# A column of ones in the rows of x and a new order of the instructions, in an induced attention followed by a rational MLP

## The chip, the cores and the metric

The kernel runs on one core of a Trainium2 chip. The core has five engines with an instruction queue each: TensorE (PE in the rows; its weight loads are PEld), VectorE (DVE), ScalarE (ACT), GpSimd (POOL) and SyncE (SP), which here issues the DMAs. The metric is the device time of one execution in microseconds.

## The reference

Four batches of N = 12,480 tokens with C = 128 channels pass two attentions over m = 32 inducing points and then an MLP with 2,048 hidden units and a rational activation:

```
mab(q, kv): s = (q @ kv.T) / sqrt(C);  a = exp(s - max(s));  a /= a.sum(-1) + 1e-9;  return a @ kv
h   = mab(inducing, x)          # 32 rows for each batch
y   = mab(x, h)                 # 12,480 rows for each batch
z   = y @ w_in                  # 128 -> 2048
g   = (a0 + a1 z + a2 z^2 + a3 z^3) / (1 + |b0| |z| + |b1| z^2 + 1e-6)
out = g @ w_out                 # 2048 -> 128
```

The change is in the first line's first use: the sum over all tokens of exp(s), by which the weighted sum of x is divided.

## The kernel before

The MLP is cut into 832 **units**: 4 batches x 26 blocks of 480 tokens x 8 pieces of 256 hidden units. A unit passes these steps:

- `first` (PE): two matmuls `h<-at,st` into one of three PSUM banks;
- the absolute value: on ACT (`rooms<-h,all`, half of the units), or for the other half, called masked, on DVE (`rooms<-h`, int32), rarely on ACT;
- for a masked unit a constant is added, either on POOL (`l<-rooms,all`, called *pre*) or by two more matmuls on PE (`h<-at,bump`, called *shift*);
- `D` (DVE): a product (`l<-h,all,l` after a pre, `l<-rooms,all,h` otherwise), after which the bank is free;
- a logarithm on ACT (`rooms<-rooms,all`): tile forms of 1,920, 3,840, 5,760 or 7,680 elements, for 1, 2, 3 or 4 pairs of units at once;
- a sigmoid on ACT: into SBUF for one unit or a pair (`rooms<-rooms` of 960 or 1,920), or into a PSUM bank (`i<-rooms`);
- the last product: on DVE (`l<-l,all,i`, when the sigmoid is in PSUM), or an add and a product on POOL;
- `second` (PE): two float32 matmuls `po<-l,w_out`, four records in the trace.

Logarithm and sigmoid have different tables on ACT, so ACT works in **rounds**: load, logarithms of some pairs, load, their sigmoids. `SIZES` says how many pairs each round has.

The attention of batch b + 1 (`induce`, `score`, `weigh`) and of the coming blocks (`tokens`) run beside the units of batch b. `score` of a **group** of four blocks gives the exponentials `e` (`e<-pc,nm` on ACT) and their transposition `eT`. `weigh` then loads the rows of x (`x_rows`, four DMAs `x<-x_t` of 256 KB into the tag `xr`) and on PE adds up, for each of 32 inducing points, exp(s) times x: 16 matmuls `ph<-x,eT` (32 records in the trace), and after them four matmuls `ph<-unit,eT` of one column (8 records), whose moving operand is a column of ones and which give the sums of exp(s) in column C of `ph`. DVE then adds `ph` to `acc`. There are 7 groups for a batch (the last of two blocks).

For batch 0 this runs before the units, in the **opening** (`boot`): there the rows come in nine wide DMAs (`rooms<-x_t`, up to 768 KB), the sums of exp(s) come from `accum_out` of the ACT instruction that makes `e`, and DVE adds them to `acc` in an instruction of their own.

The order of all instructions is fixed when the program is built. `Flow` simulates the engines with the costs of the table `COST` and picks, for each engine, the ready step with the lowest due time, which is its ready time plus a number of `RANK` or `GEN`. Those numbers change along the way: `SETS` has rows of 36 numbers, `PLAN` says which row holds in which of 52 stretches of 16 units. A job like `weigh` tells the planner what its step on an engine takes, by a yield:

```
        yield "bank", 0
        yield "pe", 0.25 * nb
        ph = self.misc(f"ph{b}_{g}")
```

Every engine runs its instructions strictly in this order. Calls of the engines go through a helper, so nearly all rows carry its line, L166; the tiles' names tell them apart.

Of the kernel before, what the change touches and what calls it, by code (L numbers as in the profile page):

```python
# [9 lines left out]
F32 = mybir.dt.float32  # L10
# [3 lines left out]
AF = mybir.ActivationFunctionType  # L14
ALU = mybir.AluOpType
PSUM = bass.MemoryType.PSUM

P = 128
TP = 120
M = 32  # L20
C = 128
HB = 4
BT = HB * TP
# [165 lines left out]
class Flow:  # L189
# [63 lines left out]
    )  # L253
    PLAN = (0, 1, 2, 3, 4, 5, 6, 7, 8, 9, 10, 11, 12, 13, 14, 15, 16, 17, 18, 19, 20, 21, 22, 23, 24, 25, 26, 27, 28, 29, 30, 31, 32, 33, 34, 35, 36, 37, 38, 39, 40, 41, 42, 43, 44, 45, 46, 47, 48, 48, 48, 48,)
    SIZES = (1, 2, 3, 4, 5, 6, 6, 6, 6, 6, 6, 6, 6, 6, 6, 6, 6, 6, 6, 6, 6, 6, 6, 6, 6, 6, 6, 6, 6, 6, 6, 6, 6, 6, 6, 6, 6, 6, 6, 6, 6, 6, 6, 6, 6, 6, 6, 6, 6, 6, 6, 6, 6, 6, 6, 6, 6, 6, 6, 6, 6, 6, 6, 6, 6, 6, 6, 6, 6, 6, 5, 3, 3)
    SWIFT = 8
    TAIL = 0.25
    MERGE = 4
# [1098 lines left out]
```

## Time and profile before

| | |
|---|---|
| time, median of 3 runs | 2217.89 us (2216.58 to 2219.45) |
| the profiled execution: time, span | 2218.13 us, 2216.2 us |
| granted TensorE clock, mean over the span | 0.988 |
| busy share PE, DVE, ACT, POOL | 96%, 92%, 95%, 86% |
| chain that ended last, by engine | PE 49%, DVE 18%, ACT 16%, POOL 9% |

Busy is the time in which an instruction of the engine was under way, as a share of the span. Matmuls are pipelined, so a busy PE may still take more work. An engine's idle time matters only where a later instruction of the chain waits for it.

### The profile page before, as it was taken

The numbers are of one execution on the slowest core, as the hardware profiler recorded it, in microseconds if no ns is written. First come the engines' busy times: TensorE is split into PE (matmuls) and PEld (weight loads), VectorE is DVE, ScalarE is ACT, GpSimd is POOL, SyncE is SP. The second block draws the span as 40 slices with busy tenths as digits, with TensorE's granted clock in tenths as the row PEclk, the third lists the DMA queues.
The fourth block names the chain that finished last, engine by engine and source line by source line (L and its number), as shares of the span: only waits on it lengthen the run. The fifth ranks groups of instructions, "written<-read, shape, count | busy, mean of one in ns | idle before, by whom it ended". The sixth has DMA issues, their size and how long they took to land.

```text
span 2216.2 us, 23881 instructions
## 1 busy us (share of the span) xinstructions
PE 2127.4 (96%) x7722; PEld 1160.0 (52%) x7722; DVE 2044.3 (92%) x2244; ACT 2112.0 (95%) x1640; POOL 1910.9 (86%) x1270
## 2 busy tenths in 40 slices
PE   6889999999999999999999999999999999999998
PEld 3545555555554555555555555555555555555554
DVE  8898999999999989999999999999999999999987
ACT  2799999999999999999999999999999999999997
POOL 0389897899999989997999999998878999999884
PEclk7899999999999999999999999999999999999999
DMA  8121122211111222222112111222110111011000
GB/s 333 51 91 58 60 82 64 65 44 45 45 36 45 75 62 82 64 80 67 45 36 63 46 58 62 73 88 73 56 61 20 45 45 45 27 38 35 27 27 20
DMA packets 76933, 135.13 MB, mean 61 GB/s; under 512 B 13312, under 2 KB 63616, under 8 KB 76800
## 3 DMA queue, kind: packets, MB, share of 16 engines
q1 hardware_dynamic: 76800, 133.52, 19.1%
q8 instruction: 64, 1.05, 0.2%
q14 instruction: 69, 0.57, 0.1%
HBM read 82.59 MB, written 25.56 MB: 49 GB/s over the span
## 4 chain that ended last, share of the span: by engine, by line
PE 49%; DVE 18%; ACT 16%; POOL 9%; issue 6%; DMA 2%; SPq 0%; DVEq 0%; ACTq 0%; POOLq 0%
PE po L166 32%; PE h L166 12%; ACT rooms L166 11%; DVE l L166 11%; POOL l L166 9%; DVE rooms L166 3%; ACT i L166 2%; PE ph L166 2%; ACT L166 2%; DMA rooms<-x_t 1%; PE pc L166 1%; DVE oT L166 1%; PE pd L166 1%; SPq L166 0%; PE pt L166 0%
## 5 line engine op out<-in xcount | busy, mean ns | idle before, releaser
L166 PE MATMUL po<-l,w_out 128*128 128x480 f32 x3328 | 1461.9, 570 | 11.6 <-DVE oT L166 8.1
L166 POOL TENSOR_TENSOR l<-l,rooms 128x960 f32<-128x960 f32 x506 | 1137.5, 2248 | 53.8 <-ACT rooms L166 16.9
L166 PEld LDWEIGHTS po<-l,w_out 128*128 128x128 f32 x3328 | 618.0, 190 | 518.9 <-issue 441.7
L166 DVE SCALAR_TENSOR_TENSOR l<-rooms,all,h 128x960 f32<-128x960 f32 x657 | 780.7, 1205 | 51.7 <-ACT rooms L166 34.1
L166 ACT ACTIVATE rooms<-rooms,all 128x1920 f32<-128x1920 f32 (+3 forms) x278 | 742.0, 2689 | 3.0 <-DVE l L166 2.5
L166 PE MATMUL h<-at,st 128*128 128x480 f32 x1664 | 629.0, 475 | 41.0 <-DVE l L166 37.5
L166 POOL TENSOR_SCALAR l<-l,all 128x960 f32<-128x960 f32 x506 | 543.7, 1075 | 1.7
L166 DVE TENSOR_SCALAR rooms<-h 128x960 int32<-128x960 int32 x413 | 473.2, 1150 | 37.6 <-PE h L166 36.3
L166 ACT ACTIVATE rooms<-rooms 128x1920 f32<-128x1920 f32 (+1 forms) x335 | 461.7, 1402 | 0.2
L166 PEld LDWEIGHTS h<-at,st 128*128 128x128 f32 x1664 | 294.7, 190 | 319.2 <-issue 163.0
L166 ACT ACTIVATE rooms<-h,all 128x960 f32<-128x960 f32 x416 | 433.6, 1052 | 21.6 <-PE h L166 19.8
L166 DVE SCALAR_TENSOR_TENSOR l<-l,all,i 128x960 f32<-128x960 f32 x326 | 385.8, 1206 | 20.5 <-ACT i L166 19.2
L166 ACT ACTIVATE i<-rooms 128x960 f32<-128x960 f32 x326 | 309.0, 964 | 12.7 <-DVE l L166 11.9
L166 POOL TENSOR_SCALAR l<-rooms,all 128x960 f32<-128x960 f32 x175 | 187.5, 1072 | 131.2 <-DVE rooms L166 112.1
L166 DVE SCALAR_TENSOR_TENSOR l<-h,all,l 128x960 f32<-128x960 f32 x175 | 210.6, 1206 | 6.7 <-POOL l L166 5.3
L166 ACT ACT_TABLE_LOAD x146 | 187.3, 1283 | 3.3 <-PEq L1350 0.7
L166 PE MATMUL h<-at,bump 128*128 128x480 f32 x482 | 179.2, 455 | 5.1 <-DVE rooms L166 5.0
L166 PEld LDWEIGHTS h<-at,bump 128*128 128x128 f32 x482 | 86.8, 190 | 78.3 <-DVE rooms L166 41.4
L166 DVE COPY oT<-po 128x480 f32<-128x480 f32 x104 | 67.6, 650 | 20.8 <-PE po L166 20.5
L166 PE MATMUL po<-at,st 128*128 128x480 f32 x104 | 78.5, 755 | 0.0
L166 POOL TENSOR_TENSOR bump<-level,bump 64x128 fp32r<-64x128 f32 x1 | 0.5, 452 | 53.3 <-DVE sum L166 53.3
L166 ACT ACTIVATE e<-pc,nm 128x480 f32<-128x480 f32 (+1 forms) x28 | 18.4, 658 | 24.4 <-DVE nm L166 21.2
(121 smaller groups left out, 763.2 us busy)
## 6 DMA issues: line engine op xcount, KB each, us to landing
xT<-x_c SPq DMA_DIRECT2D x182, 240.0 KB, 3.4
out<-oT SPq DMA_DIRECT2D x104, 240.0 KB, 2.2
at<-hl SPq DMA_DIRECT2D x412, 60.0 KB, 2.0
x<-x_t SPq DMA_DIRECT2D x78, 256.0 KB, 3.4
rooms<-x_t SPq DMA_DIRECT2D x8, 768.0 KB, 13.3
rooms<-x_c SPq DMA_DIRECT2D x5, 960.0 KB, 13.7
raw<-w_in SPq DMA_DIRECT2D x4, 480.0 KB, 8.6
raw<-w_out SPq DMA_DIRECT2D x5, 384.0 KB, 12.5
```

Of the source, the lines that this page charges most:

```text
L166: ins = call(*args, **kw)
```

## The change

The rows of x in DRAM (`x_t`) get a 129th element that is 1, so that a row of four tokens in a partition has 2,064 bytes in place of 2,048. The matmuls `ph<-x,eT` have 129 columns and so also give the sums of exp(s); the matmuls with `unit` and the tile `unit` go, and in the opening `accum_out` and DVE's own instructions for the sums go too. The planner is told another cost for the step. `SETS` and `PLAN` are replaced: 52 rows, one for each stretch, in place of 49; the last rounds of `SIZES` become 6, 2, 4, 3, 2 pairs in place of 6, 5, 3, 3. With that the order of all engines after the opening is another one.

```
     SETS = (
-        (93.1, 124, -262.9, 107.9, -98, -199.3, -83.4, 13.3, 36.9, 113.2, -213.9, 106.7, 409, 149.2, 15.7, 4.9, 67.1, 34.1, -13.5, -190.6, -1.2, 162.6, 30.3, -281.3, 0.07, 0.14, 0.03, 0.09, -1.22, -1.54, 193.8, 106.1, 40, 64.3, 281.9, 30),
+        (93.1, 124, -262.9, 107.9, -135.2, -199.3, -83.4, 13.3, 36.9, 113.2, -213.9, 106.7, 409, 149.2, 15.7, 4.9, 67.1, 34.1, -13.5, -190.6, -1.2, 162.6, 30.3, -281.3, 0.07, 0.14, 0.03, 0.09, -1.22, -1.54, 193.8, 106.1, 45.7, 64.3, 281.9, 30),
...
-        self.unit = cp.tile([P, 1], F32, name="unit")
-        nc.vector.memset(self.unit, 1.0)
...
-            t = self.ap.tile([P, HB, C], F32, tag="xr", name=f"x{b}_{n}", bufs=4)
+            t = self.ap.tile([P, HB, C + 1], F32, tag="xr", name=f"x{b}_{n}", bufs=4)
...
-            nc.scalar.activation(e[rows], pc[rows, 0:BT], AF.Exp, bias=nm[rows], scale=scale, accum_out=sums[rows])
...
+        nc.scalar.activation(e[rows], pc[rows, 0:BT], AF.Exp, bias=nm[rows], scale=scale)
...
-        yield "pe", 0.25 * nb
+        yield "pe", 0.03 + 0.27 * nb
...
-                nc.tensor.matmul(ph[M * j:M * j + M, 0:C], eT[:, c, M * j:M * j + M], xs[j][:, c, :], start=(c == 0), stop=(c == HB - 1))
...
-                V.scalar_tensor_tensor(out=acc[rows, C:], in0=acc[rows, C:], scalar=state[g][rows], in1=sums[rows], op0=ALU.mult, op1=ALU.add)
-            return
-        for c in range(HB):
-            nc.tensor.matmul(ph[rows, C:C + 1], eT[:, c, rows], self.unit[0:TP], start=(c == 0), stop=(c == HB - 1))
-        yield "unring", 0
+                nc.tensor.matmul(ph[M * j:M * j + M, 0:C + 1], eT[:, c, M * j:M * j + M], xs[j][:, c, :], start=(c == 0), stop=(c == HB - 1))
+        if not self.boot:
+            yield "unring", 0
```

In the order of TensorE, the end of the first group's sum of batch 1 (`ph_0`), and the units of block 2 behind it. Before:

```order
L166 MATMUL ph_0_1093<-x_2_1028,eT_0_1018 32x128
L166 MATMUL ph_0_1093<-x_3_1030,eT_0_1018 32x128
L166 MATMUL ph_0_1093<-unit,eT_0_1018 128x1 x4
L166 MATMUL h_2_4_1116<-at_1_1_874,st_645 128x480 x2
L166 MATMUL h_2_5_1121<-at_1_1_874,st_645 128x480 x2
L166 MATMUL po_1_2_1085<-l_1_3_972,w_out 128x480 x2
L166 MATMUL h_2_4_1116<-at_1_1_874,bump 128x480 x2
```

The same place now:

```order
L166 MATMUL ph_0_1077<-x_2_1012,eT_0_1002 32x129
L166 MATMUL ph_0_1077<-x_3_1014,eT_0_1002 32x129
L166 MATMUL h_2_4_1096<-at_1_1_858,st_629 128x480 x2
L166 MATMUL h_2_5_1102<-at_1_1_858,st_629 128x480 x2
L166 MATMUL po_1_2_1069<-l_1_3_956,w_out 128x480 x2
L166 MATMUL h_2_6_1110<-at_1_1_858,st_629 128x480 x2
L166 MATMUL h_2_4_1096<-at_1_1_858,bump 128x480 x2
```

The four matmuls with `unit` are gone, and the shift of unit 2_4 has moved behind the first matmuls of unit 2_6.

In the order of ScalarE, the end of the program: the last two rounds of batch 3's last blocks (`i` is a sigmoid into PSUM). Before:

```order
L166 ACTIVATE i_24_7_14285<-rooms 128x2x480
L166 ACTIVATE i_25_0_14290<-rooms 128x2x480
L166 ACTIVATE i_25_1_14293<-rooms 128x2x480
L166 ACT_TABLE_LOAD
L166 ACTIVATE rooms<-rooms,all 128x5760
L166 ACT_TABLE_LOAD
L166 ACTIVATE i_25_2_14315<-rooms 128x2x480
L166 ACTIVATE i_25_3_14317<-rooms 128x2x480
L166 ACTIVATE i_25_4_14322<-rooms 128x2x480
L166 ACTIVATE i_25_5_14327<-rooms 128x2x480
L166 ACTIVATE i_25_6_14330<-rooms 128x2x480
L166 ACTIVATE i_25_7_14335<-rooms 128x2x480
```

The same place now:

```order
L166 ACTIVATE i_24_7_14195<-rooms 128x2x480
L166 ACTIVATE i_25_0_14198<-rooms 128x2x480
L166 ACTIVATE i_25_1_14203<-rooms 128x2x480
L166 ACTIVATE i_25_2_14206<-rooms 128x2x480
L166 ACTIVATE i_25_3_14212<-rooms 128x2x480
L166 ACT_TABLE_LOAD
L166 ACTIVATE rooms<-rooms,all 128x3840
L166 ACT_TABLE_LOAD
L166 ACTIVATE i_25_4_14229<-rooms 128x2x480
L166 ACTIVATE i_25_5_14233<-rooms 128x2x480
L166 ACTIVATE i_25_6_14236<-rooms 128x2x480
L166 ACTIVATE i_25_7_14241<-rooms 128x2x480
```

The last round has two pairs of units in place of three: the sigmoids of units 25_2 and 25_3 stand a round earlier.

Over the whole program, as the order lists them, these counts change beside those of the sum itself: the logarithms of 1, 2, 3 and 4 pairs from 187, 56, 23 and 12 to 173, 58, 25 and 13; table loads from 146 to 148; sigmoids into SBUF of one unit and of a pair from 164 and 171 to 159 and 175, into PSUM from 326 to 323; matmuls of the shift from 482 to 512; POOL's *pre* from 175 to 160; the absolute value of masked units on ACT from 3 to 1; of ACT's copies out of PSUM (`eT`, `a`, `hl`, `gs`) three, three and two fewer and four more, DVE taking or giving them.

## Rows read from the trace of the kernel before

**Rows 1.** The page: busy time by engine, and one group of weight loads.

```profile
PE 2127.4 (96%) x7722; PEld 1160.0 (52%) x7722; DVE 2044.3 (92%) x2244; ACT 2112.0 (95%) x1640; POOL 1910.9 (86%) x1270
...
L166 PEld LDWEIGHTS po<-l,w_out 128*128 128x128 f32 x3328 | 618.0, 190 | 518.9 <-issue 441.7
```

**Rows 2.** Busy time by stretch; columns PE, PEld, DVE, ACT, POOL, clock, DMA.

```profile
105.00:2204.00 2099.00, 2041.96 (x7204) 1111.34 (x7203) 1955.72 (x1982) 2064.94 (x1572) 1891.06 (x1248) 1.00 0.18 54
```

**Rows 3.** The timeline of PE from 121.5 us: start, length, work.

```profile
122.11 1.08 PE L166 MATMUL ph<-x,eT 120*32 120x128 f32 x32
...
123.12 1.05 PE L166 MATMUL ph<-unit,eT 120*128 120x1 f32 x8
...
124.04 1.12 PE L166 MATMUL h<-at,st 128*128 128x480 f32 x4
```

**Rows 4.** Groups by form on PE: count, busy, mean ns, idle before.

```profile
L166 PE MATMUL ph<-unit,eT 120*64 120x1 f32 x24 | 1.9, 200 | 0.0
...
L166 PE MATMUL h<-at,bump 128*128 128x480 f32 x482 | 179.2, 455 | 5.1 <-DVE rooms L166 5.0
```

**Rows 5.** Groups by form on ACT.

```profile
L166 ACT ACTIVATE rooms<-rooms,all 128x1920 f32<-128x1920 f32 x187 | 350.0, 1894 | 2.8 <-DVE l L166 2.5
...
L166 ACT ACTIVATE i<-rooms 128x960 f32<-128x960 f32 x326 | 309.0, 964 | 12.7 <-DVE l L166 11.9
...
L166 ACT ACTIVATE rooms<-rooms 128x1920 f32<-128x1920 f32 x171 | 304.3, 1795 | 0.2
...
L166 ACT ACTIVATE rooms<-rooms,all 128x3840 f32<-128x3840 f32 x56 | 195.8, 3496 | 0.1
...
L166 ACT ACT_TABLE_LOAD x146 | 187.3, 1283 | 3.3 <-PEq L1350 0.7
...
L166 ACT ACTIVATE rooms<-rooms 128x960 f32<-128x960 f32 x164 | 162.7, 992 | 0.0
...
L166 ACT ACTIVATE rooms<-rooms,all 128x5760 f32<-128x5760 f32 x23 | 117.3, 5099 | 0.1
...
L166 ACT ACTIVATE rooms<-rooms,all 128x7680 f32<-128x7680 f32 x12 | 80.4, 6702 | 0.0
...
L166 ACT ACTIVATE eT<-pt 120x512 f32<-120x512 f32 x10 | 5.9, 592 | 9.4 <-PE pt L166 9.4
```

**Rows 6.** The chain of waits at the end: start, length, work.

```profile
2198.59 0.98 ACT i L166
...
2199.60 1.22 DVE l L166
...
2200.86 10.16 PE po L166 x25
```

**Rows 7.** The timeline of ACT at the end.

```profile
2198.59 5.48 ACT L166 ACTIVATE i<-rooms 128x960 f32<-128x960 f32 x6
```

**Rows 8.** Busy time in the 6 us after each of the 21 groups.

```profile
sum 126.00, PE 124.05 PEld 79.13 DVE 106.22 ACT 119.03 POOL 112.42; mean PE 5.91 PEld 3.77 DVE 5.06 ACT 5.67 POOL 5.35
```

**Rows 9.** Waits of DVE from 105 us: total, times, longest.

```profile
DVE acc L166 <- PE ph L166: 6.9, 9, 1.1
...
DVE l L166 <- PE h L166: 10.4, 19, 2.4
```

**Rows 10.** Groups by form on POOL.

```profile
L166 POOL TENSOR_SCALAR l<-rooms,all 128x960 f32<-128x960 f32 x175 | 187.5, 1072 | 131.2 <-DVE rooms L166 112.1 <-PE h L166 7.2 <-PE po L166 5.2
```

**Rows 11.** Tile x, its transfers.

```profile
DMA to landing us min/median/max: 2.6/3.4/5.0
```

**Rows 12.** The timeline of SP before one group's sum.

```profile
979.13 1.89 SPq L166 DMA_DIRECT2D x<-x_t  x4
```

**Rows 13.** The timeline of PE at that group's sum.

```profile
986.19 1.08 PE L166 MATMUL ph<-x,eT 120*32 120x128 f32 x32
```

**Rows 14.** The chain of waits in the opening.

```profile
10.91 14.03 DMA rooms<-x_t
...
25.02 13.67 DMA rooms<-x_t
```

More of the change, by code (lines that the diff above doesn't have):

```diff
@@ L203 @@
     SETS = (
[49 rows of a table removed]
-    )
-    PLAN = (0, 1, 2, 3, 4, 5, 6, 7, 8, 9, 10, 11, 12, 13, 14, 15, 16, 17, 18, 19, 20, 21, 22, 23, 24, 25, 26, 27, 28, 29, 30, 31, 32, 33, 34, 35, 36, 37, 38, 39, 40, 41, 42, 43, 44, 45, 46, 47, 48, 48, 48, 48,)
-    SIZES = (1, 2, 3, 4, 5, 6, 6, 6, 6, 6, 6, 6, 6, 6, 6, 6, 6, 6, 6, 6, 6, 6, 6, 6, 6, 6, 6, 6, 6, 6, 6, 6, 6, 6, 6, 6, 6, 6, 6, 6, 6, 6, 6, 6, 6, 6, 6, 6, 6, 6, 6, 6, 6, 6, 6, 6, 6, 6, 6, 6, 6, 6, 6, 6, 6, 6, 6, 6, 6, 6, 5, 3, 3)
[52 rows of a table added]
+    )
+    PLAN = (0, 1, 2, 3, 4, 5, 6, 7, 8, 9, 10, 11, 12, 13, 14, 15, 16, 17, 18, 19, 20, 21, 22, 23, 24, 25, 26, 27, 28, 29, 30, 31, 32, 33, 34, 35, 36, 37, 38, 39, 40, 41, 42, 43, 44, 45, 46, 47, 48, 49, 50, 51,)
+    SIZES = (1, 2, 3, 4, 5, 6, 6, 6, 6, 6, 6, 6, 6, 6, 6, 6, 6, 6, 6, 6, 6, 6, 6, 6, 6, 6, 6, 6, 6, 6, 6, 6, 6, 6, 6, 6, 6, 6, 6, 6, 6, 6, 6, 6, 6, 6, 6, 6, 6, 6, 6, 6, 6, 6, 6, 6, 6, 6, 6, 6, 6, 6, 6, 6, 6, 6, 6, 6, 6, 6, 2, 4, 3, 2)
     SWIFT = 8
@@ L695, in x_rows @@
         if self.boot:
-            t = self.mp.tile([P, HB, C], F32, tag=self.place("l"), name=f"x{b}_{n}", bufs=1)
+            t = self.mp.tile([P, HB, C + 1], F32, tag=self.place("l"), name=f"x{b}_{n}", bufs=1)
         else:
-            t = self.ap.tile([P, HB, C], F32, tag="xr", name=f"x{b}_{n}", bufs=4)
+            t = self.ap.tile([P, HB, C + 1], F32, tag="xr", name=f"x{b}_{n}", bufs=4)
         self.nc.sync.dma_start(out=t, in_=self.x_t[b, :, HB * n:HB * n + HB, :])
@@ L702, in x_columns @@
     def x_columns(self, b, n):
-        t = self.ap.tile([C, HB * C], F32, tag="xr", name=f"xT{b}_{n}", bufs=4)[:, 0:BT]
+        t = self.ap.tile([C, HB * (C + 1)], F32, tag="xr", name=f"xT{b}_{n}", bufs=4)[:, 0:BT]
         self.nc.sync.dma_start(out=t, in_=self.x_c[b, :, BT * n:BT * n + BT])
@@ L722, in wide_rows @@
         n, m = 3 * k, min(3, self.NB - 3 * k)
-        t = self.room().rearrange("p a b n -> p (a b n)")[:, 0:m * HB * C].rearrange("p (m h c) -> p m h c", h=HB, c=C)
+        t = self.room().rearrange("p a b n -> p (a b n)")[:, 0:m * HB * (C + 1)].rearrange("p (m h c) -> p m h c", h=HB, c=C + 1)
         self.nc.sync.dma_start(out=t.rearrange("p m h c -> p (m h) c"), in_=self.x_t[b, :, HB * n:HB * (n + m), :])
@@ L755, in score @@
         e = ap.tile([P, BT], F32, tag="e", name=f"e{b}_{g}")
-        if self.boot:
-            state["sum", g] = sums = ap.tile([P, 1], F32, tag="sums", name=f"sums{b}_{g}", bufs=3)
-            nc.scalar.activation(e[rows], pc[rows, 0:BT], AF.Exp, bias=nm[rows], scale=scale, accum_out=sums[rows])
-        else:
-            nc.scalar.activation(e[rows], pc[rows, 0:BT], AF.Exp, bias=nm[rows], scale=scale)
+        nc.scalar.activation(e[rows], pc[rows, 0:BT], AF.Exp, bias=nm[rows], scale=scale)
         yield "free", 0
@@ L784, in weigh @@
             for j in range(nb):
-                nc.tensor.matmul(ph[M * j:M * j + M, 0:C], eT[:, c, M * j:M * j + M], xs[j][:, c, :], start=(c == 0), stop=(c == HB - 1))
-        if self.boot:
-            V, sums = nc.vector, state["sum", g]
-            if g == 0:
-                V.tensor_copy(out=acc[:, 0:C], in_=ph[:, 0:C])
-                V.tensor_copy(out=acc[:, C:], in_=sums)
-            else:
-                V.scalar_tensor_tensor(out=acc[rows, 0:C], in0=acc[rows, 0:C], scalar=state[g][rows], in1=ph[rows, 0:C], op0=ALU.mult, op1=ALU.add)
-                V.scalar_tensor_tensor(out=acc[rows, C:], in0=acc[rows, C:], scalar=state[g][rows], in1=sums[rows], op0=ALU.mult, op1=ALU.add)
-            return
-        for c in range(HB):
-            nc.tensor.matmul(ph[rows, C:C + 1], eT[:, c, rows], self.unit[0:TP], start=(c == 0), stop=(c == HB - 1))
-        yield "unring", 0
+                nc.tensor.matmul(ph[M * j:M * j + M, 0:C + 1], eT[:, c, M * j:M * j + M], xs[j][:, c, :], start=(c == 0), stop=(c == HB - 1))
+        if not self.boot:
+            yield "unring", 0
         yield "v", 0.26
@@ L1340 @@
     arrays = {
-        "x_t": np.pad(x.reshape(B, N // TP, TP, C).transpose(0, 2, 1, 3), ((0, 0), (0, P - TP), (0, 0), (0, 0))),
+        "x_t": np.pad(np.pad(x.reshape(B, N // TP, TP, C).transpose(0, 2, 1, 3), ((0, 0), (0, 0), (0, 0), (0, 1)), constant_values=1), ((0, 0), (0, P - TP), (0, 0), (0, 0))),
         "x_c": x.transpose(0, 2, 1),
```

97 rows, old and new, of the table SETS are left out of this document.

## Prediction

> **What bounds the kernel now.** First the page: four engines are busy between 86% and 96% of the span, so no share alone says which one sets the end [rows 1]. PE's 96% counts pipelined matmuls. How full it really is shows where `po` runs without a break: 25 records in 10.16 us, 0.406 us each [rows 6]. At that pace the 3,328 records of `po` take 1,352 us; the 1,664 of `h` and 482 of the shift at no less than 0.28 us (four in 1.12) take another 601 [rows 3, 4]. That is 1,953 of 2,216 us before the 2,248 smaller records: PE has a few per cent of room.
>
> Then the stretch in which units run, 105 to 2204 us: ACT idles 2099.0 - 2064.9 = 34 us there, PE by its busy time 57, DVE 143, POOL 208 [rows 2]. ACT has the least room: 1.6%, spread over a thousand and a half instructions. I take ACT's work as the bound, and the other engines as what makes the 34 us of gaps. So the change is worth what it takes from ACT's work, plus what it takes from ACT's gaps, plus the end, after ACT's last instruction.
>
> The Trainium skill, in Trainium Kernel Development and Optimization, section Performance Expectations, calls matmul busy time a bad metric of the distance to the roofline, and the busy share of weight loads a good one. By that rule PE, at 52%, would be half free, the removed matmuls would be worth nothing, and the sum below would end at 2211.7. The trace does not bear it out: in `po` without a break a weight load of 0.19 us stands in each 0.406 us, 47%, so 52% is what a full PE shows in this kernel [rows 1, 6].
>
> **The sum's matmuls on PE.** With four blocks the eight records with `unit` stand between 123.12 and the next matmul at 124.04 us: 0.92 us [rows 3]. The last group of a batch has two blocks: 1.9 us in three groups, 0.63 each [rows 4]. So 18 x 0.92 + 3 x 0.63 = 18.4 us of PE go. The 129th column adds 1/128 of 1.0 us in 21 groups, 0.2 us. Against it stand 30 more matmuls of the shift, between 0.28 us [rows 3] and 0.372 us (179.2 / 482) [rows 4] each: 8.4 to 11.2 us. PE is 7 to 10 us lighter. None of this is on ACT, so it counts only through gaps (below).
>
> **ACT's work.** Logarithms: 14 fewer of 1.894 us, two more of 3.496, two more of 5.099, one more of 6.702: -26.5 + 7.0 + 10.2 + 6.7 = -2.6 us. Sigmoids: five fewer of 0.992, four more of 1.795, three fewer of 0.964: -0.7. Two more table loads of 1.283: +2.6. Four fewer copies on balance at the 0.592 of `eT`: -2.4; two fewer absolute values, at the 0.964 of the nearest form: -1.9 [rows 5]. Sum: -5.0 us. DVE takes over copies and absolute values, and does three products fewer; its 143 us of idle time cover that. If that cover were gone, these 4.3 us would come back as waits.
>
> **The end.** After the last table load the chain is a sigmoid (0.98), DVE's product (1.22), then `po`, 25 records for six units and the linear part [rows 6]. With four units it has 17 records: 10.16 - 8 x 0.406 = 6.91, 3.25 us less. ACT's own part after that load falls too, from six sigmoids (5.48) to four (3.65), 1.83 us [rows 7], since two of them now stand before it. Measured from the end of ACT's work, the program ends 3.25 - 1.83 = 1.4 us earlier: -1.4. The price is already in ACT's sum, as two table loads.
>
> **ACT's gaps.** In the 6 us behind the 21 blocks of `unit` matmuls ACT is busy 119.03 of 126 us: 7.0 us idle [rows 8], where 1.6% would be 2.0. So at most 4.9 us are put down to these blocks. DVE waits 6.9 us for `ph` itself, nine times, which must nearly vanish [rows 9]. The planner counted 0.25 x 4 = 1.0 us for the step and PE took 1.93 (122.11 to 124.04) [rows 3]; now it counts 1.11 and the rest lasts 1.01, so order and chip agree better. Some of the 4.9 belongs to what follows a group anyway. I take half, -2.5; the ends are 0 and -4.9.
>
> **POOL.** It loses 15 constants of 1.07 us [rows 10] and has 208 us idle: worth nothing by itself. But D of these 15 units now waits for a PE queue. The trace before shows D waiting for PE 10.4 us in all, 19 times, the longest 2.4 [rows 9]; with 241 shifted units that is 0.04 us each. Ends: 0 to 15 x 2.4 = 36 us; I take 0.6, nothing, by that mean.
>
> **Transfers.** Rows of x are 16 bytes longer in 2,048. The four loads of a group land after 2.6 to 5.0 us [rows 11]. In one of the tightest groups their last is issued at 981.0 and PE needs it at 986.2 [rows 12, 13]: covered by a fraction of a microsecond to 2 us, and 0.8% of 3.4 us is 0.03. Nothing waits. In the opening two wide transfers of 14.03 and 13.67 us stand on the chain [rows 14]: 0.8% of 27.7 is +0.2 us, and DVE's and ACT's saved sum instructions give about that back. I take 0. The two equal transfers differ by 0.36, so the ends are -0.7 and +0.7.
>
> A rule speaks against the longer rows: the Trainium skill, in DMA: Bandwidth & Descriptors, section How a descriptor splits into AXI transactions, cuts a descriptor at 256-byte boundaries. By it an aligned row of 2,048 bytes is eight transactions and one of 2,064 bytes that starts at odd multiples of 16 nine; a wide row goes from 24 to 25, an estimated +1.2 us in the opening, and the sum would be 2210.4. No row of before has such a start, so no run shows it yet.
>
> **The sum**, against the profiled execution: 2218.1 - 5.0 - 1.4 - 2.5 = 2209.2 us. It lies 0.2 us over the median of the runs shown, so this holds for both: 2209.
>
> **Rivals.** *Hidden.* The PE time was never waited for, and the 15 shifted units wait at the mean of an actual wait, 10.4 / 19 = 0.55 us, which ACT then feels: 2218.1 - 5.0 - 1.4 + 8.2 = 2219.9, no change. For it: most of the 21 blocks are followed by little ACT idle time. Against it: 222 of the 241 shifted units wait for nothing today.
>
> *The whole block.* Each block held up every engine by its full length, because the order behind it was planned 0.9 us too early and nothing made that good: 2218.1 - 6.4 - 18.4 = 2193.3. For it: PE's small room. Against: the idle time behind the blocks holds only 4.9 us of this.
>
> *Slower: the shift behind `second`.* A shift stands on PE behind whole units of `po`, 4 x 0.406 = 1.62 us; the order shows it one step further back for unit 2_4. If D of each of the 15 units waits that long, and ACT behind it, the cost is 24.4 us: 2209.2 + 24.4 = 2233.6. It decides from 8.9 / 15 = 0.6 us for each of them. For it: waits of up to 2.4 us occur. Against: PE is lighter, and the mean of all shifted units is 0.04.
>
> **How the numbers follow.** Chances: the forecast 0.62, hidden 0.19, the whole block 0.09, the slower one 0.10. The forecast's own range is 2203 to 2214: the gaps' two ends, the opening's, and as much again for a new order's own gaps. A measurement of this kernel tells 0.2%, 4.4 us, from no change, so faster means under 2213.5. Faster: 0.62 x 0.9 + 0.09 = 0.65, rounded to 0.64; same: 0.19 and the rest of the forecast, 0.25; slower 0.11, with a little of the hidden case. The range takes in half of the whole-block case's way and just passes the hidden case: 2199 to 2221.
>
> **What would show it.** Right: ACT busy near 2107 us in all; its idle time between 105 us and its end at 34 us or under, and nothing but 2.0 us of it behind the sums; no `unit` group, DVE's wait for `ph` near 0; at the end a `po` of 17 records in 6.9 us; x landing at 3.4 us. Wrong: the same ACT work with more idle time, and the waits of D for PE above 10.4 us (the slower case) or of ACT for D; x landing late enough that PE waits for it; an opening whose wide transfers are a microsecond longer.

## The result: 18 us faster, twice the forecast

The changed kernel takes 2199.53 us (median of 4 runs, 2196.61 to 2200.82) and the kernel before 2217.27 in the runs beside it: a ratio of 0.9916 [0.9899, 0.9934]. The forecast was 2209; the time lies at the low edge of the range. The profiled executions, 2218.13 and 2199.38 us, are 18.75 apart.

The page of the changed kernel, parts 1, 3 and one line of part 6, answers to [rows 1] and [rows 11]:

```profile
PE 2119.9 (96%) x7584; PEld 1146.1 (52%) x7584; DVE 2042.3 (93%) x2239; ACT 2105.8 (96%) x1616; POOL 1902.4 (87%) x1261
...
q1 hardware_dynamic: 76800, 133.73, 19.3%
...
x<-x_t SPq DMA_DIRECT2D x78, 258.0 KB, 3.5
```

Every engine has less work, and the shares still don't say which one decides. Where the time went can be booked on ACT, as the forecast did: the stretch from 105 us to the end of ACT's last instruction holds its work and its gaps. This doesn't say yet which engine made the gaps. First the kernel before, then the one after (columns as in [rows 2]):

```profile
105.00:2204.07 2099.07, 2042.03 (x7204) 1111.34 (x7203) 1955.79 (x1982) 2065.00 (x1572) 1891.06 (x1248) 1.00 0.18 54
```

```profile
105.00:2186.53 2081.53, 2034.93 (x7071) 1097.85 (x7071) 1955.04 (x1986) 2059.56 (x1555) 1882.88 (x1239) 1.00 0.18 55
```

ACT's work falls by 2065.00 - 2059.56 = 5.4 us. Its gaps fall from 2099.07 - 2065.00 = 34.1 to 2081.53 - 2059.56 = 22.0, by 12.1. The chain of waits at the end, answering to [rows 6]:

```profile
2181.59 1.28 ACT L166
...
2182.88 0.98 ACT i L166
2183.86 0.03 issue
2183.89 1.23 DVE l L166
2185.11 0.04 issue
2185.16 6.93 PE po L166 x17
```

The last `po` has 17 records in 6.93 us. From ACT's end the program takes 2197.3 - 2186.5 = 10.8 us, before (2216.24 - 2204.07) 12.2: 1.4 less. The three parts, 5.4 + 12.1 + 1.4 = 18.9, are the difference of the spans. The opening gives nothing: by the chain of waits the units begin at 105.23 us, before at 104.96.

So two of the three terms came out as forecast. The gaps did not: -12 for -2.5. ACT's waits that shrank, after, from 105 us (total, times, longest):

```profile
ACT rooms L166 <- PE h L166: 8.7, 16, 2.2
...
ACT i L166 <- DVE l L166: 4.9, 13, 0.9
```

Before they were these:

```profile
ACT rooms L166 <- PE h L166: 14.0, 25, 2.2
ACT i L166 <- DVE l L166: 11.9, 21, 2.1
```

Together 12.3 us less. Neither wait names `ph` or the sums.

### The profile page after: what moved, and what is told of

Its sections match the earlier page's. It is cut to its first block, busy times and chain, and to the rows that moved or that the text cites. A ratio compares the mean times of both kernels' runs of the same rounds, so it can differ in the third digit from the quotient of the medians.

```text
span 2197.3 us, 23539 instructions
## 1 busy us (share of the span) xinstructions
PE 2119.9 (96%) x7584; PEld 1146.1 (52%) x7584; DVE 2042.3 (93%) x2239; ACT 2105.8 (96%) x1616; POOL 1902.4 (87%) x1261
## 3 DMA queue, kind: packets, MB, share of 16 engines
q1 hardware_dynamic: 76800, 133.73, 19.3%
## 4 chain that ended last, share of the span: by engine, by line
PE 44%; POOL 18%; ACT 16%; DVE 14%; issue 6%; DMA 3%; SPq 1%; POOLq 0%; DVEq 0%; ACTq 0%
PE po L166 28%; POOL l L166 17%; ACT rooms L166 11%; PE h L166 11%; DVE l L166 8%; DVE rooms L166 3%; ACT i L166 2%; DMA rooms<-x_t 2%; ACT L166 2%; PE ph L166 1%; SPq L166 1%; PE pl L166 1%; DVE oT L166 1%; PE pc L166 1%; PE pt L166 0%
## 5 line engine op out<-in xcount | busy, mean ns | idle before, releaser
L166 PE MATMUL po<-l,w_out 128*128 128x480 f32 x3328 | 1465.6, 570 | 11.5 <-DVE oT L166 7.2
L166 DVE SCALAR_TENSOR_TENSOR l<-rooms,all,h 128x960 f32<-128x960 f32 x672 | 798.9, 1206 | 49.3 <-ACT rooms L166 28.0
L166 ACT ACTIVATE rooms<-rooms 128x960 f32<-128x960 f32 (+1 forms) x334 | 463.7, 1413 | 0.2
L166 DVE SCALAR_TENSOR_TENSOR l<-l,all,i 128x960 f32<-128x960 f32 x323 | 382.5, 1208 | 22.7 <-ACT i L166 21.9
L166 POOL TENSOR_SCALAR l<-rooms,all 128x960 f32<-128x960 f32 x160 | 170.8, 1068 | 114.7 <-DVE rooms L166 108.4
L166 DVE SCALAR_TENSOR_TENSOR l<-h,all,l 128x960 f32<-128x960 f32 x160 | 193.2, 1209 | 9.0 <-POOL l L166 7.5
L166 PE MATMUL h<-at,bump 128*128 128x480 f32 x512 | 189.8, 453 | 2.5 <-DVE rooms L166 2.5
L166 PEld LDWEIGHTS h<-at,bump 128*128 128x128 f32 x512 | 92.9, 189 | 71.0 <-DVE rooms L166 30.9
L166 DVE COPY oT<-po 128x480 f32<-128x480 f32 x104 | 67.8, 652 | 18.4 <-PE po L166 18.2
L166 ACT ACTIVATE e<-pc,nm 128x480 f32<-128x480 f32 (+1 forms) x28 | 18.4, 656 | 23.1 <-DVE nm L166 19.9
```

Source lines behind the costliest of these rows:

```text
L166: ins = call(*args, **kw)
```

## The experiments

**The two halves apart.** `e1_drop_only` is the changed kernel with the order of before; `e2_order_only` is the kernel before in the new order, with its `unit` matmuls and rows of 2,048 bytes.

```
e1, against after:                         e2, against before:
-    SETS, PLAN, SIZES of after            -    SETS, PLAN, SIZES of before
+    SETS, PLAN, SIZES of before           +    SETS, PLAN, SIZES of after
-        yield "pe", 0.03 + 0.27 * nb      -        yield "pe", 0.25 * nb
+        yield "pe", 0.25 * nb             +        yield "pe", 0.03 + 0.27 * nb
```

> Before's order, instruction for instruction after the opening, without the matmuls with unit (rows of x with the column of ones, the opening's sums as in the change). Three theories for the 12 us that went from ACT's gaps. Blocks: the 0.92 us blocks themselves made these gaps, so taking them out of the old order gives 10 to 12 us: about 2206 us. Order: the new numbers made the gaps smaller, the blocks only 2 to 5 us: 2212 to 2215. Agreement: the old order was planned for a step of 1.0 us; without the blocks the chip does what was planned, 5 to 10 us: 2207 to 2212.

> The new order, instruction for instruction after the opening, with the matmuls with unit put back behind each sum and rows of x of 128 elements; the planner still counts 1.11 us for the step, so the blocks come unplanned. Blocks: 10 to 12 us of the change's 18 are lost: 2209 to 2212. Order: 2 to 5 us are lost: 2202 to 2205. Agreement: 5 to 10 us: 2205 to 2210. Beside that, PE's waits for x, 3.8 us in the new kernel: with rows of 2,048 bytes they go if the longer rows made them, and stay if the new order issues the loads too late.

Beside a median of 2217.06 us for the kernel before, e1 takes 2202.49 us (2201.50 to 2206.64, 5 runs), 0.9936 [0.9923, 0.995]; e2 takes 2212.38 (2210.63 to 2215.22, 11 runs), 0.9977 [0.9968, 0.9986]. Without the blocks of `unit` the old order is 14.6 us faster. The new order with the blocks is 4.7 faster. In the new order the blocks cost 2212.4 - 2199.5 = 12.9 us. They are the larger part of the gain in either order, and both figures lie above the 10 to 12 us that the theory of the blocks gave. A little of the 14.6 is TensorE's clock: e1's runs have a granted clock of 0.992 in the median, those of the kernel before beside it 0.989. Between runs at 0.992 the difference is about 13.7 us (2202.22 and 2202.49 against 2215.88 and 2216.30). e1 also has the change's opening; its first sum starts 0.6 us earlier than before (121.5 for 122.1 us).

The order of e1 is that of before, so the two can be laid side by side, instruction by instruction. PE from 1436 us before:

```profile
1436.29 1.08 PE L166 MATMUL ph<-x,eT 120*32 120x128 f32 x32
1437.30 1.05 PE L166 MATMUL ph<-unit,eT 120*128 120x1 f32 x8
1438.22 1.86 PE L166 MATMUL po<-l,w_out 128*128 128x480 f32 x4
1439.54 0.97 PE L166 MATMUL h<-at,st 128*128 128x480 f32 x2
```

The same place in e1:

```profile
1424.84 1.09 PE L166 MATMUL ph<-x,eT 120*32 120x129 f32 x32
1425.86 1.88 PE L166 MATMUL po<-l,w_out 128*128 128x480 f32 x4
1427.37 0.80 PE L166 MATMUL h<-at,st 128*128 128x480 f32 x2
```

PE is 11.45 us ahead at `ph` and 12.36 at the `po` behind it. ACT there before, and in e1:

```profile
1437.84 1.89 ACT L166 ACTIVATE rooms<-rooms,all 128x1920 f32<-128x1920 f32 x1
1440.61 1.06 ACT L166 ACTIVATE rooms<-h,all 128x960 f32<-128x960 f32 x1 [0.87 <-PE h L166]
```

```profile
1426.41 1.89 ACT L166 ACTIVATE rooms<-rooms,all 128x1920 f32<-128x1920 f32 x1
1428.27 1.06 ACT L166 ACTIVATE rooms<-h,all 128x960 f32<-128x960 f32 x1
```

Before, ACT waits 0.87 us for `h`, the second job behind the block; without the block it doesn't wait. The whole block comes back within 4 us. The next group, at 1485.9 us, has the same price elsewhere. ACT before, and in e1:

```profile
1501.88 1.28 ACT L166 ACT_TABLE_LOAD   x1
1503.81 0.97 ACT L166 ACTIVATE i<-rooms 128x960 f32<-128x960 f32 x1 [0.64 <-DVE l L166]
```

```profile
1489.32 1.28 ACT L166 ACT_TABLE_LOAD   x1
1490.62 0.97 ACT L166 ACTIVATE i<-rooms 128x960 f32<-128x960 f32 x1
```

Here ACT pays 0.64 us, 18 us behind the block, at a wait that names DVE. Taken so for all 21 groups (each instruction's start before, less its start in e1), ACT's lead grows by these sums, counted from just ahead of each block:

```
us behind the block       2      6     12     20     30    next block
ACT's lead, 21 groups   1.2    6.6   11.5   13.5   14.3   14.3
```

Of the 14.3 us, 6.6 are gained in the first 6 us and 7.7 later. Three groups end with nothing or a loss (123, 746 and 1,600 us), and behind the last of them the lead falls from 14.9 to 11.5 us; this execution of e1, 2206.64 us, is the longest of its five.

Not all of this is the blocks. For a few microseconds at a time the granted TensorE clock was at the lower of its two levels (0.50, 1.2 GHz), at places that differ between the two executions. Before, and then in e1 (columns as in [rows 2]):

```profile
822.10:825.40 3.30, 3.30 (x6) 1.45 (x5) 3.30 (x4) 3.19 (x3) 1.07 (x1) 0.50 0.00 0
```

```profile
135.30:142.00 6.70, 6.42 (x15) 2.42 (x16) 5.93 (x6) 5.53 (x6) 6.53 (x5) 0.50 0.35 104
1712.30:1715.60 3.30, 3.30 (x7) 1.72 (x6) 2.00 (x3) 3.30 (x4) 3.22 (x3) 0.50 0.08 29
```

PE had idled 0.80, 0.45 and 0.35 us in the last microseconds before the fall at 822 us, and 2.06 us just before the one at 1712. The group at 809 us has 2.6 of the 14.3 us, and 1.7 of that come at ACT's waits between 827 and 837 us, behind the low clock of before. The first group's loss lies at the low clock of e1 from 135 us on, where before has 0.75 on the mean. Of the 3.4 us lost behind the last group, 1.1 lie just ahead of the fall at 1712 us and 1.3 behind it. The 19 groups other than those at 123 and 809 us gain 12.9 us, 5.8 of them in the first 6 us, so the reading holds without these two: more than half is paid later.

**The planner's numbers.** `e3_old_numbers` is the changed kernel with the `SETS`, `PLAN` and `SIZES` of before but the new cost; `e10_other_course` is the changed kernel with 0.01 us more in that cost; `e4_true_cost` is the kernel before with the `unit` block counted.

```
e3, against after:   SETS, PLAN, SIZES of before
e10, against after:
-        yield "pe", 0.03 + 0.27 * nb
+        yield "pe", 0.04 + 0.27 * nb
e4, against before:
-        yield "pe", 0.25 * nb
+        yield "pe", 0.03 + 0.27 * nb + 0.92 * nb / 4
```

> The change without the new numbers: matmuls with unit gone, cost 0.03 + 0.27 nb, but SETS, PLAN and SIZES of before, so the planner makes another order from the first sum on. Blocks: 2206. Agreement: at least as good as the old order without the blocks, 2205 to 2210. Order (the numbers are fitted to one course of the planner, and any shift of it spoils them): slower than the old order without the blocks by 5 to 20 us, 2217 to 2235.

> The new kernel with one cost of the planner 0.01 us higher: the step of the sum is planned at 0.04 + 0.27 nb. Numbers, data and instructions as in the change; from the first difference on the planner takes another course. If the new numbers are good because cost and chip agree: 2197 to 2205. If they are good for one course of the planner only, as the old numbers with another cost suggest (2291 and 2308): 2230 to 2300.

> Before with one number changed: the step of the sum is planned at its measured length (1.11 + 0.92 us for four blocks) in place of 1.0; blocks, numbers and data as before. Agreement: faster than before by 3 to 6 us, 2211 to 2214. Blocks: 2217. Order: the numbers no longer fit the planner's course, 2220 to 2240.

All three are far slower, e3 and e4 beyond every range given and e10 within its second: e3 2290.73 us, 1.0334 [1.032, 1.0348]; e10 2264.73, 1.0212 [1.0198, 1.0226]; e4 2307.79, 1.041 [1.0395, 1.0424]. The page of e10, and its longest wait of ACT:

```profile
PE 2140.7 (95%) x7564; PEld 1143.0 (50%) x7564; DVE 2032.2 (90%) x2229; ACT 2119.0 (94%) x1650; POOL 1934.2 (85%) x1283
```

```profile
ACT rooms L166 <- PE h L166: 26.1, 34, 2.4
```

ACT has 34 instructions and 2119.0 - 2105.8 = 13.2 us of work more than after. The rest of the 65 us is its gaps and a longer end. The granted clock fell as well: over the span it was 0.983 in e10, 0.982 in e3 and 0.971 in e4, for 0.990 in after, so part of these gaps may be a slower TensorE; how much isn't measured. The numbers fit one course of the planner, and 0.01 us in one cost leads it onto another. So these three say that the numbers must be searched anew for such a change of a cost. They can't say whether a cost nearer the chip's makes a better order: the course changes with it. That part of my forecast's reasoning stays open.

**What a microsecond that the planner doesn't know costs.** `e8_blocks_twice` issues the `unit` matmuls of before twice; `e5_act_block`, `e6_dve_block` and `e7_pool_block` add two instructions of useless work to each group of the changed kernel, on one engine, unknown to the planner, 42 in all. The order of everything else stays.

```
e8 (before):       the loop of matmul(ph[rows, C:C + 1], eT[:, c, rows], self.unit[0:TP], ...) a second time
e5 (after, ACT):   + nc.scalar.activation(self.scratch, self.w_in[:, 384 * k:384 * k + 384], AF.Identity, ...)
e6 (after, DVE):   + nc.vector.scalar_tensor_tensor(out=self.scratch[:, 0:320], in0=self.w_in[...], in1=self.w_in[:, 0:320], ...)
e7 (after, POOL):  + nc.gpsimd.tensor_scalar(out=self.scratch, in0=self.w_in[:, 384 * k:384 * k + 384], ...)
```

> Before, with the matmuls with unit issued twice behind each sum (the first four are written over): another 18 us of PE in the old order. If PE's time is passed on in proportion, as its removal was: 2217 + 14 = 2231, to 2235 if nothing more is hidden. If the first block filled what room there was before: the full 18.4, 2235. If blocks hurt only up to some length: 2220 to 2225.

> The new kernel and its order, with a useless copy on ScalarE, two instructions of about 0.47 us, behind each of the 21 sums: 19 to 20 us of ACT that the planner doesn't know. If ACT alone is the bound (my step): all of it is paid, 2217 to 2220. If any unplanned work on any engine is passed on for about 0.7 of its length (as PE's 18.4 us were: 12.9 in the new order, 14 in the old): 2212 to 2215.

> The same with two products of 128 x 320 on VectorE, about 0.9 us together, 19 us in all. ACT alone: DVE idles 130 us, so little is paid, 2200 to 2204. Any engine: 0.7 of it, 2211 to 2214.

> The same with two instructions of 128 x 384 on GpSimd, about 0.9 us together, 19 us in all. POOL idles 180 us, most of all engines. ACT alone: 2200 to 2203. Any engine: 2208 to 2214. Only the engines whose busy share leaves under 3% (ACT, PE): 2200 to 2203 here and on VectorE.

The groups by form show how long the added work is (count, busy, mean ns, idle before), in e5, e6 and e7:

```profile
L166 ACT ACTIVATE scratch<-w_in 128x384 f32<-128x384 f32 x42 | 21.8, 518 | 0.7
```

```profile
L166 DVE SCALAR_TENSOR_TENSOR scratch<-w_in 128x320 f32<-128x320 f32 x42 | 53.2, 1266 | 0.7
```

```profile
L166 POOL TENSOR_SCALAR scratch<-w_in 128x384 f32<-128x384 f32 x42 | 21.6, 515 | 1.8
```

| | work, us | time, us | ratio to before | over its base, us | per us of work |
|---|---|---|---|---|---|
| e1, PE, removed | -17.8 | 2202.49 | 0.9936 [0.9923, 0.995] | -14.6 | 0.8 |
| e8, PE, doubled | 17.4 | 2239.61 | 1.0104 [1.0088, 1.012] | 23.1 | 1.3 |
| e5, ACT | 21.8 | 2217.26 | 0.9995 [0.9986, 1.0004] | 17.7 | 0.8 |
| e6, DVE | 53.2 | 2243.46 | 1.0119 [1.0104, 1.0135] | 43.9 | 0.8 |
| e7, POOL | 21.6 | 2205.95 | 0.9946 [0.9933, 0.996] | 6.4 | 0.3 |

The base is after (2199.53), for e1 and e8 the kernel before (2217.06 and 2216.54 in their runs). PE's work is what the traces show from `ph` to the matmul behind the blocks: 0.90 us less in e1 for a group of four blocks and 0.54 for one of two, 0.89 and 0.47 more in e8. PE, ACT and DVE pass four fifths of such work on, or more. DVE does so with 2081.5 - 1955.0 = 126 us of idle time in the same stretch, and PE, in the kernel before, with 2099.1 - 2042.0 = 57. So idle time is not room here. That the cause is a fixed order with little slack between steps fits ACT's lead above, but the slack itself was not measured. Only POOL hides most.

e5 alone would fit my step that ACT is the bound (2217 to 2220 expected). e6 rules it out: by that step DVE's work would have cost 0 to 5 us. e6 isn't DVE's work alone, though: its products wait for POOL, as the last section shows, and POOL's own work takes 1908.7 us there for 1902.4 after. e8 passes its longest range, 2235 us. In its trace the first group alone delays ACT by 4.3 us, where the granted clock is 0.50 from 139.6 to 146.3 us; most of the other groups of four delay it by about their 0.89. Whether the doubled blocks brought the low clock isn't shown.

**A small thing taken out.** `e9_no_add` is the changed kernel without POOL's addition of 1e-9 to the tokens' softmax sums, which are at least 1, where it changes nothing in float32: 28 instructions of 7.0 us in all in the trace of after.

```
-        (nc.vector if self.boot else nc.gpsimd).tensor_scalar(out=sm, in0=sm, scalar1=1e-9, ...)
+        if self.boot:
+            nc.vector.tensor_scalar(out=sm, in0=sm, scalar1=1e-9, ...)
```

> The new kernel without GpSimd's addition of 1e-9 to the token softmax's sums (27 instructions, 6.9 us; the sums are at least 1, so the float32 result is the same), all else and the order unchanged. If GpSimd's time is worth 0.30 of its length, as the block put in there cost: -2 us, 2197.5. If it is worth nothing on the side of removal: 2199.5. If the wait of VectorE's reciprocal for GpSimd counts beside it: 2194 to 2196.

2200.12 us (2195.71 to 2201.30), 0.9922 [0.9909, 0.9936]: no difference from after. A gain was expected and none is seen. By e7's 0.3 the 7.0 us would be worth 2 us, within what five runs spread over. No kernel here has a median under that of the changed kernel.

## Why the prediction was wrong

- **The bound.** Wrong. I took ACT's work as the bound, with PE and DVE behind cover. A microsecond that PE or DVE is held costs as much as one of ACT (e1, e5, e6).
- **The matmuls on PE.** Right in size: e1's PE leads by 0.90 us more at each group of four blocks, for the 0.92 worked out, and by 0.54 at one of two, for 0.63: 17.8 us in all for 18.4 less 0.2. "It counts only through gaps" was right too; the gaps were mis-sized.
- **ACT's gaps.** This is the step that failed: -2.5 forecast, with -4.9 as its far end, and -12.1 measured; e1 has 2087.6 - 2062.4 = 25.2 us of gaps, so -8.9 of it, in its longest execution. Three faults lie in it. I counted idle time only in the 6 us behind a block [rows 8], and 7.7 of 14.3 us are paid later (7.1 of 12.9 without the two groups beside a low clock). I took off 2.0 us as what stands behind any instruction, but of the 7.0 us there e1 gave back 6.6. And I halved what was left for caution, with no row behind the half. The rival "the whole block" had the mechanism: 18.4 us in full, of which e1 gave 14.6 and e2 against after 12.9. I gave it 0.09 because of the idle time behind the blocks; the window of 6 us was the fault there as well.
- **ACT's work, -5.0, and the end, -1.4.** Right: -5.4 and -1.4. As time the order is worth less than these 6.4: 4.7 us in e2 and 2202.49 - 2199.53 = 3.0 between e1 and after, where the intervals of the two ratios overlap. Part of it may go into gaps: e2 has 37.1 us of them (2202.5 - 105 - 2060.4), 3.0 more than before, but in its longest execution, 2.8 us over its median.
- **POOL and the shift.** Right at 0 as far as the runs tell. D's wait for `h` [rows 9] rose from 10.4 to 15.0 us, 19 to 29 times, 0.3 us for each of the 15 units, and in e2 to 15.1, so it is the order's. The slower rival needed 0.6 each.
- **Transfers.** Right in the sum, though "nothing waits" was not: PE now idles 3.8 us before `ph` for x, eight times, by the view of the tile x; e2 has 2.4, seven times, with rows of 2,048 bytes, so most comes with the order, and e1 has none with rows of 2,064.
- **The rule on transactions.** The Trainium skill's rule (DMA: Bandwidth & Descriptors, How a descriptor splits into AXI transactions) does not show in the trace: packets of the row loads took a median of 84 ns at 2,048 bytes and 85 at 2,064, where nine transactions for eight would be 12% more. The queue's share went from 19.1% to 19.3% of a span that is 0.9% shorter, with 0.2% more bytes.
- **The rule on weight loads.** Taken as the measure of PE's room, the Trainium skill's rule (Trainium Kernel Development and Optimization, Performance Expectations) would have made the removed matmuls worth nothing. e1 measured 14.6 us for them. That price by itself doesn't show a full PE, since in e6 DVE passed work on with 126 us idle; what speaks against the rule is the 47% in `po` without a break.

## What to carry to other kernels

In a program whose in-order engines all run above 85% and wait for each other in turn, price unplanned work by most of its length or all of it on any of the tight engines (0.8 to 1.3 here, 0.3 on POOL), and look for what it costs far behind it, at waits that don't name it. Idle time next to the instruction was a lower bound here (7.0 us of the 14.3), and an engine's sum of idle time was not cover. A list of numbers that was searched for one planner's costs can be worth nothing for another cost, even one 0.01 us away (65 us here): change the work, then search again, and test the work alone in the old order.

## What the runs showed of the hardware

In e6 the added product on DVE, 128x320 with both operands in SBUF, took 0.48 to 2.42 us. DVE and POOL there, around the first:

```profile
122.19 2.70 DVE L166 SCALAR_TENSOR_TENSOR scratch<-w_in 128x320 f32<-128x320 f32 x2
```

```profile
121.77 2.25 POOL L166 TENSOR_TENSOR l<-l,rooms 128x960 f32<-128x960 f32 x1
125.20 1.05 POOL L166 TENSOR_TENSOR a<-a,asm 120x512 f32<-120x512 f32 x1 [1.18 <-DVE asm L166]
```

The first of the two started at 122.19 and lasted 2.18 us, until 0.35 us after POOL's product had ended at 124.02; the second, with POOL idle, took 0.49. The Trainium skill, in SBUF — State Buffer, section Who interferes with whom, has a DVE instruction with two inputs in SBUF contend with a GpSimd instruction that reads SBUF, for a shared pair of ports that is locked; these rows agree with it. The kernel's own products on DVE have one operand in PSUM, and the 323 with the sigmoid take 1,208 ns on the mean. That is how e6's 42 small products came to 53.2 us of work, and its cost per microsecond counts DVE's time in that wait as work.
